# Two-dimensional Fourier mixing and an RWKV channel mix on one core: an earlier load gate and a new order of batch 1's loads

## The chip, the cores and the metric

The kernel runs on one core of a Trainium2 chip. The metric is the time of one execution on the device in microseconds. Times are given as the median of several runs; one further execution is profiled, and all rows of profile and trace come from that one.

## The reference, cut to what matters

The input x has 8 batches of 3072 rows (sequence) and 256 columns. The first stage takes the real part of a Fourier transform over both axes; the second is an RWKV channel mix over the result.

```python
X = np.fft.fft(x, axis=1)
X = np.fft.fft(X, axis=2)
x = X.real.astype(np.float32)

x_prev = np.concatenate([np.zeros((B, 1, D)), x[:, :-1, :]], axis=1)
xk = mu_k * x + (1.0 - mu_k) * x_prev
xr = mu_r * x + (1.0 - mu_r) * x_prev
k = np.maximum(xk @ w_k, 0.0)              # w_k: 256 x 1024
v = k * k @ w_v                            # w_v: 1024 x 256
r = 1.0 / (1.0 + np.exp(-(xr @ w_r)))      # w_r: 256 x 256
return r * v
```

## The kernel before, in words

**The mixing stage.** The kernel works through the batches one by one. As the input is real, only about half of the transform has to be computed, and the mirrored half follows from it. For each batch and each half h of the rows, `load_xh(b, h)` brings x from memory twice: `load_p` (L136, and L133 for batches from 2 on) brings rows in their order into a tile `xp`, and `load_m` (a gather by row numbers, L139, through the helper `gather`) brings the mirrored rows into `xm`. Half 0 has one more small gather of its own, `load_m0`. `fold(b, h)` (L168 and L170, on DVE) adds the two into `p`. Then come matrix products with tables of cosines and sines: `a_sum` (L574), or `butterfly` on DVE (L179) with `a_item` behind it (L533, L530); `d_units` (L596); `turned` (L619); `c_sums` (L637). They give `y`, the spectrum of the batch.

**The channel mix.** `diff` (L690) forms the difference of neighbouring rows, and `mix_part` or `mix` (L702, L713, L729, and L885 for the very first piece) forms the mixed inputs: `x00` and `x01` for K (first and mirrored half of the rows) and `x10`, `x11` for R. A batch has six chunks of 512 rows, three for each half m. For each chunk there are four pieces `k_piece` (PE, L748, with the relu on ACT, L758), squares (DVE, L768, or ACT, L766), `r_item` (PE, L775, with the sigmoid on ACT, L780), the second product (`v_part`, L801, for the first four chunks and `v_tile`, L789, after that), and `v_out` (DVE, L811), which multiplies by r and starts the stores on SP's queue (L819).

**The weights.** For half m of the rows the weights are `wk_sb[m]` (two tiles of 128x1024), `wr_sb[m]` (two of 128x256); `wv_sb` is shared. They are gathered by the row numbers in `row_i`, as the mirrored half needs them in another order of rows. `loads()` brings `wk_sb[0]` and `wv_sb`; `loads_1()` brings `wr_sb[0]`, and batch 1's two halves; `loads_2()`, called in step 4, makes the tables of row numbers for the later batches and brings `wk_sb[1]` and `wr_sb[1]`.

**What sets the order.** All loads named so far are issued from POOL's queue, in the order in which the program names them; POOL computes each load's list, so issuing takes it time too. Every engine's instructions run in the order of the program (`pin_order`). A list of steps is written out by hand: in step n PE gets one piece of K, then the step's other products, then parts of the second product; in the same step come the DVE work (`at(...)`) and the `v_out` that are due. Chunk 0 has the K pieces of steps 0 to 3, chunk 1 those of 4 to 7, and so on; `r_item` of chunk 0 stands in step 5, `fold(1, 0)` in step 4, `fold(1, 1)` in step 11, `v_part` of chunk 0 in steps 3 to 6, its `v_out` in step 6, `v_part` of chunk 1 from step 7. The second product has two slots of PSUM in all (`ps_v`), each of them for two blocks of 128 rows; `v_out` frees them. The other products share three slots (`ps_w`).

**The gate.** `load_gate` holds POOL's queue until DVE has come to a certain place: DVE sets one element to zero, and POOL's next instruction writes that element.

```python
def load_gate():
    V.memset(gate, 0)
    iota(gate, pattern=[[0, 1]], base=0, channel_multiplier=0)
```

So loads that the program names after the gate start no earlier than DVE's memset (L451) and POOL's iota (L452). Before the first gate, `loads()` has issued the first K weights and `wv_sb`; its `dma_start` is the last thing that POOL does until the gate.

`keep_busy(n, ps)` runs n products with zeros on PE; the numbers stand in `NF = (9, 0, 0, 3, 0, 3, 0)`, so that `NF[1]` and `NF[2]` are 0.

Of the kernel before, what the change touches and what calls it, by code (L numbers as in the profile page):

```python
# [20 lines left out]
def _v(ap, extra_offset, free_dims):  # L21
    new_ap = [list(ap.ap[0])] + [[s, c] for (s, c) in free_dims]
    return dataclasses.replace(ap, offset=ap.offset + extra_offset, ap=new_ap)
# [16 lines left out]
def kernel(  # L40
# [37 lines left out]
    def ps_w():  # L78
        return ps_slot("W", 3, 1024)

    def ps_v():
        return ps_slot("V", 2, 512)
# [35 lines left out]
    def x_tiles(b, h):  # L118
        xp_t[b, h] = xp_sb[(2 * b + h - 1) % 3] if b or h else xp_00
        xm_t[b, h] = xm_sb[(2 * b + h) % 3]  # L120
# [3 lines left out]
    def parts(b):  # L124
        return 112 if b > 1 else 96

    def load_p(b, h):
        r, n = 9 * h, 9 - h
        if b > 1:
            for g in range(2):  # L130
                src = dataclasses.replace(x[b, 32 * g + r:32 * g + r + 1, :],
                                          ap=[[64 * D, N1], [D, n], [1, D]])
                nc.gpsimd.dma_start(out=xp_t[b, h][64 * g:64 * g + N1, 0:n], in_=src)  # L133
            return
        src = dataclasses.replace(x[b, r:r + 1, :], ap=[[32 * D, 96], [D, n], [1, D]])
        nc.gpsimd.dma_start(out=xp_t[b, h][0:96, 0:n], in_=src)  # L136

    def gather(dst, src, idx):
        nc.gpsimd.indirect_dma_start(dst, None, src, bass.IndirectOffsetOnAxis(ap=idx, axis=0))  # L139

    def load_m(b, h, o, n, idx):
        gather(xm_t[b, h][0:parts(b), XM0 + o:XM0 + o + 256 * n],
               x.rearrange("b (s r) d -> (b s) (r d)", r=n), idx)

    def load_m0(b):
        if b == 0:
            gather(xm_00[:, 1:257], x.rearrange("b s d -> (b s) d"), idx_0[:, 0:1])
        else:
            load_m(b, 0, 2048, 1, (idx_g0 if b > 1 else idx_0)[:, b:b + 1])

    def load_xh(b, h):
        x_tiles(b, h)
        load_p(b, h)
        if h == 0:
            load_m0(b)
        load_m(b, h, 0, 8, (idx_g8 if b > 1 else idx_8)[:, b, h:h + 1])

    def fold(b, h, q0=0, n=0):

        n = n or 9 - h  # L160
        if (b, h) not in p_t:
            p_t[b, h] = p_pool.tile([112, 9, 256], FP16, name="p")
        k = parts(b)
        p, xp, xm = p_t[b, h][0:k], xp_t[b, h][0:k], xm_t[b, h][0:k]
        o = XM0 + 256 * (8 - h - q0)
        if (b, h, q0) == (0, 0, 0):
            xm, o = xm_00, 1
        V.tensor_tensor(out=p[:, q0:q0 + n], in0=xp[:, q0:q0 + n],  # L168
                        in1=_v(xm, o + 256, [(-256, n), (-1, 256)]), op=ALU.add)
        V.tensor_tensor(out=p[:, q0:q0 + n, 0], in0=xp[:, q0:q0 + n, 0],  # L170
                        in1=_v(xm, o, [(-256, n)]), op=ALU.add)
# [28 lines left out]
    def keep_busy(n, ps, cols=512):  # L200

        for _ in range(n):
            nc.tensor.matmul(out=ps[:, 0:cols], lhsT=zeros,
                             rhs=_v(zeros, 0, [(0, cols // P), (1, P)]), start=True, stop=True)

    fill = ps_w()
    keep_busy(4, fill)
    NF = (9, 0, 0, 3, 0, 3, 0)
# [72 lines left out]
    def rv(n, o, *dims, k=1):  # L281
        return _v(rw_0[0:k], P * n + o, list(dims)) if n < 6 else _v(rw_1, P * (n - 6) + o, list(dims))
# [45 lines left out]
    def outer(out, *pairs):  # L328
        for n, (row, r) in enumerate(pairs):
            nc.tensor.matmul(out=out, lhsT=row, rhs=r, start=n == 0, stop=n == len(pairs) - 1)  # L330
# [45 lines left out]
    ang_ps = [ps_v(), ps_v()]  # L376
# [46 lines left out]
    def rows():  # L423
        for a in range(2):
            for half in range(2):
                iota(_v(row_i[64 * half:64 * half + 64], a, [(3 - 2 * a, 2)]), pattern=[[0, 2]],
                     base=256 * a + half * (1 - 2 * a), channel_multiplier=2 - 4 * a)
        iota(row_i[0:1, 2:3], pattern=[[0, 1]], base=0, channel_multiplier=0)
        iota(_v(row_i[0:1], 1, [(2, 2)]), pattern=[[0, 2]], base=128, channel_multiplier=0)
# [11 lines left out]
    def loads():  # L441
        rows()
        for a in range(2):
            gather(wk_sb[0][a], moe_w_k, row_i[:, a:a + 1])
        nc.gpsimd.dma_start(out=wv_sb, in_=moe_w_v.rearrange("(fc p) v -> p fc v", p=128))
# [4 lines left out]
# [3 lines that stand above are left out]

    def loads_1():
        load_gate()
        for a in range(2):
            gather(wr_sb[0][a], moe_w_r, row_i[:, a:a + 1])
        load_xh(1, 0)
        load_xh(1, 1)

    def loads_2():
        for lo in (0, 64):
            k = slice(lo, 64 if lo == 0 else 112)
            iota(idx_g8[k], pattern=[[S // 8, B], [-1, 2]], base=S // 8 - 1 - lo // 16,
                 channel_multiplier=-8)
            iota(idx_g0[k], pattern=[[S, B]], base=S - lo // 2, channel_multiplier=-64)
        iota(idx_g0[0:1], pattern=[[S, B]], base=0, channel_multiplier=0)
        for a in range(2):
            gather(wk_sb[1][a], moe_w_k, row_i[:, 2 + a:3 + a])
        for a in range(2):  # L470
            gather(wr_sb[1][a], moe_w_r, row_i[:, 2 + a:3 + a])

# [36 lines left out]
    def evac(out_ap, in_ap, eng):  # L509
        if eng == "V":  # L510
            V.tensor_copy(out=out_ap, in_=in_ap)
        else:
            nc.scalar.activation(out=out_ap, in_=in_ap, func=AF.Copy)  # L513

    def a_tile(b):
        a_t[b] = y_pool.tile([P, 2, NU, 64], FP16, name="a")
# [45 lines left out]
    def a_sum(b, h, i0, eng="A", m=4):  # L562


        if (h, i0) == (0, 0):
            a_tile(b)
        ps = ps_w() if m == 4 else ps_v()
        for i in range(m):
            parts = [(h, i0 + i + 1 - h, 0, 2 * WA, 0, 1)]
            if h and i0 + i == 7:  # L570
                parts = [(0, 0, 0, WA, WA, 1), (1, 7, 1, WA, 1, 2)]
            for half, q, o, n, w, step in parts:
                for k in range(2):
                    nc.tensor.matmul(out=_v(ps, 256 * i + o, [(2 * WA // n, n)]),  # L574
                                     lhsT=p_t[b, half][0:96, q, 128 * k:128 * k + 128],
                                     rhs=_v(w_pm[0:96], (WA + WB) * k + w,
                                            [(WA + WB, 2), (step, n // 2)]),
                                     start=(k == 0), stop=(k == 1))
        a_ps[b, h, i0] = ps
        if eng:  # L580
            a_evac(b, h, i0, eng, m)
# [3 lines left out]
    def a_evac(b, h, i0, eng, m=4):  # L585
        evac(_v(a_t[b], 8 * h + i0, [(16, 2 * WA), (1, m)]),
             _v(a_ps[b, h, i0], 0, [(1, 2 * WA), (256, m)]), eng)
# [12 lines left out]
    def d_evac(ps, u0, n, bank, eng):  # L600
        evac(_v(g_all, 256 * u0, [(64, 2), (128, 2 * n), (1, 64)]),
             _v(ps, 0, [(bank, 2), (64, 2 * n), (1, 64)]), eng)
# [234 lines left out]
        outer(mu_ps[:, 4 + n:5 + n], (tv(TO + n, 0, (1, P)), rv(ONE, 0, (1, 1))))  # L837
    for k in range(2):
        outer(mu_ps[:, 64 + NU * k:64 + NU * k + NU], (rw_h[:, k], rv(JR, 0, (1, NU))))
    a_sum(0, 0, 0)  # L840
    fold(0, 0, 5, 4)
    a_sum(0, 0, 4)
    half_tables(mu_ps)
    V.tensor_copy(out=muf_t, in_=mu_ps[:, 0:6])
    loads()
    fold(0, 1, 0, 4)
    a_sum(0, 1, 0, "A")
    fold(0, 1, 4, 4)
# [8 lines left out]
    fill = ps_w()  # L857
# [16 lines left out]
    turned(2, 4, small[1][:, 256:258], "V")  # L874
    d_evac(fill[:, 256:1024], 4, 1, 512, "A")
    d_evac(fill[:, 384:1024], 5, 1, 512, "V")
    x_t[0, 0, 0] = mix_pool.tile([P, 2, 1536], FP16, name="x00")
    for a in range(2):
        t = x_t["t", a] = mix_pool.tile([P, 24, 64], FP16, name=f"t{a}")
# [3 lines left out]
    for a in range(2):  # L883
        for z in range(2):
# [2 lines left out]
                                   scalar=mu_f[:, a, 0:1],  # L887
                                   in1=_v(x_t["t", a], 64 * z, [(128, 2), (1, 64)]),
                                   op0=ALU.mult, op1=ALU.add)
    loads_1()  # L890
    y, odd = y_t[0], ps_v()
    even = ps_v()
    for f in range(2):
# [60 lines left out]
    event(3, (turned, 8, 13))  # L954
    event(4, (c_item, 0, 17, 8))
    at(4, loads_2)
    at(4, fold, 1, 0)
    at(5, r_item, (0, 0, 0))
# [158 lines left out]
```

## Time and profile before

| | us |
|---|---|
| median of 3 runs | 437.23 |
| lowest and highest run | 435.13 and 437.72 |
| the profiled execution | 439.32 |
| its span in the trace | 437.2 |
| PE busy | 425.7 (97%) |
| DVE busy | 361.5 (83%) |
| ACT busy | 321.6 (74%) |
| POOL busy | 63.8 (15%) |

The profile is of one execution. PE is TensorE's products and PEld its weight loads, DVE is VectorE, ACT is ScalarE, POOL is GpSimd, SP only issues DMAs here. Rows of the timeline have the start, the length in us, the engine, the line of the kernel, the operation, what it writes and reads, and how often; in brackets stands how long the engine had been idle before it, and what ended that. A row can stand for several instructions of one kind. The chain of waits is followed back from the last instruction of the stretch to what released it, step by step. In the windows each row is a stretch of time with the busy time of each engine in it (and the number of instructions), then the clock that TensorE was granted as a share of the full one, the busy share of the DMA engines and what they moved.

The mean granted clock of the whole execution was 0.992.

### The profile page before, as it was taken

The numbers are of one execution on the slowest core, as the hardware profiler recorded it, in microseconds if no ns is written. First come the engines' busy times: TensorE is split into PE (matmuls) and PEld (weight loads), VectorE is DVE, ScalarE is ACT, GpSimd is POOL, SyncE is SP. The second block draws the span as 40 slices with busy tenths as digits, with TensorE's granted clock in tenths as the row PEclk, the third lists the DMA queues.
The fourth block names the chain that finished last, engine by engine and source line by source line (L and its number), as shares of the span: only waits on it lengthen the run. The fifth ranks groups of instructions, "written<-read, shape, count | busy, mean of one in ns | idle before, by whom it ended". The sixth has DMA issues, their size and how long they took to land.

```text
span 437.2 us, 9304 instructions
## 1 busy us (share of the span) xinstructions
PE 425.7 (97%) x3853; PEld 299.7 (69%) x3853; DVE 361.5 (83%) x560; ACT 321.6 (74%) x375; POOL 63.8 (15%) x89
## 2 busy tenths in 40 slices
PE   8897999999999999999999999999999999999996
PEld 3564776777677777677767767776777776767675
DVE  8769889988898988989799888989889847997543
ACT  7695888787877777786787778777777867666661
POOL 7288401000041000500014000410000000000000
PEclk9898999999999999999999999999999999999999
DMA  7889953633259222863339332682322323233333
GB/s 133 118 132 194 202 99 58 120 73 73 49 111 190 60 56 68 143 148 69 71 58 189 94 73 62 111 189 50 70 63 64 70 53 72 52 71 73 73 73 97
DMA packets 34990, 41.81 MB, mean 96 GB/s; under 512 B 4098, under 2 KB 31076, under 8 KB 34948
## 3 DMA queue, kind: packets, MB, share of 16 engines
q1 hardware_dynamic: 27380, 24.92, 23.4%
q0 software_dynamic: 7264, 16.04, 22.6%
q8 instruction: 30, 0.49, 0.5%
q10 hardware_dynamic: 304, 0.26, 0.2%
q14 instruction: 12, 0.10, 0.1%
HBM read 32.08 MB, written 25.17 MB: 131 GB/s over the span
## 4 chain that ended last, share of the span: by engine, by line
PE 91%; DMA 3%; DVE 2%; POOL 1%; issue 1%; ACT 0%; DVEq 0%; ACTq 0%
PE psW L748 37%; PE psV L789 36%; PE psW L775 9%; DMA xm<-in_x_dram,idx 3%; PE psW L596 2%; PE psV L801 2%; PE psW L669 1%; PE psW L556 1%; PE psW L574 1%; PE psW L637 0%; DVE p L168 0%; POOL xm L139 0%; POOL wr L139 0%; PE psV L574 0%; DVE k L768 0%
## 5 line engine op out<-in xcount | busy, mean ns | idle before, releaser
L758 ACT ACTIVATE rl<-psW 128x1024 f16<-128x1024 f32 x192 | 195.3, 1025 | 95.7 <-PE psW L748 91.9
L748 PE MATMUL psW<-x,wk 128*128 128x512 f16 (+1 forms) x776 | 196.3, 378 | 0.5
L789 PE MATMUL psV<-wv_sb,k 128*128 128x256 f16 x1424 | 184.1, 273 | 0.0
L789 PEld LDWEIGHTS <-k 128*128 128x128 f16 x1424 | 136.9, 98 | 35.7
L768 DVE TENSOR_TENSOR k<-rl 128x2048 f16<-128x2048 f16 (+1 forms) x101 | 116.2, 1151 | 33.5 <-ACT rl L758 33.0
L748 PEld LDWEIGHTS <-wk 128*128 128x128 f16 x776 | 75.1, 98 | 54.0 <-issue 1.8
L811 DVE SCALAR_TENSOR_TENSOR o<-psV,r 128x512 f32<-128x512 f32 (+1 forms) x97 | 65.7, 680 | 16.0 <-PE psV L789 13.5
L713 DVE TENSOR_TENSOR x<-y,t 128x1536 f16<-128x1536 f16 (+2 forms) x72 | 61.6, 860 | 2.1
L775 PE MATMUL psW<-wr,x 128*128 128x256 f16 x384 | 49.8, 273 | 0.0
L780 ACT ACTIVATE r<-psW 128x1024 f16<-128x1024 f32 x48 | 48.9, 1019 | 0.8 <-PE psW L775 0.8
L775 PEld LDWEIGHTS <-x 128*128 128x128 f16 x384 | 37.5, 98 | 14.3 <-issue 0.2
L452 POOL IOTA gate<- 1x1 int32 x6 | 2.1, 356 | 205.1 <-DVE gate L451 205.1
L513 ACT ACTIVATE a<-psW 128x832 f16<-128x832 f32 x31 | 26.1, 863 | 3.2 <-PE psW L574 1.8
L139 POOL DMA_INDIRECT xm<-in_x_dram,idx_g x18 | 26.2, 1455 | 5.5 <-issue 5.2
L513 ACT ACTIVATE g_all<-psW 128x1024 f16<-128x1024 f32 (+5 forms) x37 | 25.6, 695 | 0.4 <-PE psW L619 0.2
L168 DVE TENSOR_TENSOR p<-xp,xm 112x2304 f16<-112x2304 f16 (+5 forms) x19 | 21.0, 1106 | 4.7 <-DMA xm<-in_x_dram,idx 4.7
L702 DVE TENSOR_SCALAR t<-d,muf_t 128x1536 f16<-128x1536 f16 (+2 forms) x40 | 20.7, 528 | 0.0
L702 DVE TENSOR_SCALAR t<-d,mu_m 128x1536 f16<-128x1536 f16 x32 | 19.6, 613 | 0.0
L801 PE MATMUL psV<-wv_sb,k 128*128 128x256 f16 x112 | 15.7, 283 | 3.0 <-DVE o L811 3.0
L596 PEld LDWEIGHTS <-a 128*128 128x128 f16 x208 | 14.1, 98 | 6.4 <-issue 0.4
L179 DVE TENSOR_TENSOR eo<-p 112x1152 f16<-112x1152 f16 (+3 forms) x28 | 17.8, 678 | 0.0
L513 ACT ACTIVATE pq<-psW 128x1024 f16<-128x1024 f32 (+1 forms) x18 | 15.2, 879 | 2.3 <-PE psW L669 2.3
(138 smaller groups left out, 221.3 us busy)
## 6 DMA issues: line engine op xcount, KB each, us to landing
out_dram<-o SPq DMA_DIRECT2D x189, 128.0 KB, 2.4
xp<-in_x_dram POOLq DMA_DIRECT2D x12, 216.0 KB, 4.6
xp<-in_x_dram POOLq DMA_DIRECT2D x12, 192.0 KB, 7.1
xp<-in_x_dram POOLq DMA_DIRECT2D x2, 432.0 KB, 5.2
xp<-in_x_dram POOLq DMA_DIRECT2D x2, 384.0 KB, 7.2
wv_sb<-in_moe_w_v_dram POOLq DMA_DIRECT2D x1, 512.0 KB, 8.2
xm<-in_x_dram,idx_g POOLq DMA_INDIRECT x18, 8.0
out_dram<-o ACTq DMA_DIRECT2D x1, 128.0 KB, 2.9
```

What stands on the lines that cost most here:

```text
L139: nc.gpsimd.indirect_dma_start(dst, None, src, bass.IndirectOffsetOnAxis(ap=idx, axis=0))
L513: nc.scalar.activation(out=out_ap, in_=in_ap, func=AF.Copy)
L702: V.tensor_scalar(out=dst, in0=src, scalar1=mu, scalar2=None, op0=ALU.mult)
L713: V.tensor_tensor(out=_v(x_t[b, j, m], o, [(64 * step, hi - lo), (step, 64)]), in0=y_t[b][:, lo + 3 * m:hi + 3 * m, a], in1=x_t["t", a][:, ...
L748: nc.tensor.matmul(out=st["k", ds][:, 512 * hs + lo:512 * hs + hi], lhsT=wk_sb[m][a][:, 128 * fc:128 * fc + 128], rhs=xk[:, a, 512 * i + l ...
L758: nc.scalar.activation(out=st["rl"][:, 2 * ds:2 * ds + 2], in_=st["k", ds].rearrange("p (f t) -> p f t", f=2), func=AF.Relu, bias=0.0, sca ...
L768: V.tensor_tensor(out=k2_t[c][:, lo:hi], in0=r, in1=r, op=ALU.mult)
L775: nc.tensor.matmul(out=ps[:, 256 * tb:256 * tb + 256], lhsT=x_t[b, 1, m][:, a, 512 * i + 128 * tb: 512 * i + 128 * tb + 128], rhs=wr_sb[m] ...
L780: nc.scalar.activation(out=st["r", c], in_=ps, func=AF.Sigmoid)
L789: nc.tensor.matmul(out=st["v", tb - h][:, 256 * h:256 * h + 256], lhsT=k2_t[c][:, fc, 128 * tb:128 * tb + 128], rhs=wv_sb[:, fc], start=(f ...
L801: nc.tensor.matmul(out=st["v", tb - h][:, 256 * h:256 * h + 256], lhsT=k2_t[c][:, fc, 128 * tb:128 * tb + 128], rhs=wv_sb[:, fc], start=fc ...
L811: V.scalar_tensor_tensor(out=o.rearrange("p a b -> p (a b)")[:, 0:256 * n], in0=st["v", t0][:, 0:256 * n], scalar=16.0, in1=st["r", c][:, ...
```

## The change

The first gate and batch 1's first half are issued ahead of the first mix (the `scaled` pieces on ACT and the four operations of L885 on DVE) instead of behind it. Within that, `load_xh(1, 0)` stands ahead of the gathers of `wr_sb[0]`. `load_xh(1, 1)` moves from there into `loads_2`, between the gathers of `wk_sb[1]` and those of `wr_sb[1]`. Two calls of `keep_busy` with the numbers `NF[1]` and `NF[2]` are added, which issue nothing, as both numbers are 0. The order of the instructions on PE and ACT stays the same; on DVE only the gate's memset moves, ahead of L885; POOL has the same instructions in the new order.

```diff
     def loads_1():
         load_gate()
+        load_xh(1, 0)
         for a in range(2):
             gather(wr_sb[0][a], moe_w_r, row_i[:, a:a + 1])
-        load_xh(1, 0)
-        load_xh(1, 1)
 
     def loads_2():
...
         for a in range(2):
             gather(wk_sb[1][a], moe_w_k, row_i[:, 2 + a:3 + a])
+        load_xh(1, 1)
         for a in range(2):
             gather(wr_sb[1][a], moe_w_r, row_i[:, 2 + a:3 + a])
...
+    keep_busy(NF[1], fill)
     a_sum(0, 0, 0)
...
     loads()
+    keep_busy(NF[2], ang_ps[1])
     fold(0, 1, 0, 4)
...
     d_evac(fill[:, 256:1024], 4, 1, 512, "A")
     d_evac(fill[:, 384:1024], 5, 1, 512, "V")
+    loads_1()
     x_t[0, 0, 0] = mix_pool.tile([P, 2, 1536], FP16, name="x00")
...
                                    op0=ALU.mult, op1=ALU.add)
-    loads_1()
     y, odd = y_t[0], ps_v()
```

## The prediction

> **What bounds the kernel now.** I read the page first: how busy each engine is over the whole span.
>
> ```profile
> span 437.2 us, 9304 instructions
> PE 425.7 (97%) x3853; PEld 299.7 (69%) x3853; DVE 361.5 (83%) x560; ACT 321.6 (74%) x375; POOL 63.8 (15%) x89
> ```
>
> PE has work in 425.7 of 437.2 us, so an edit that only moves loads can win no more than the 11.5 us in which PE is idle, and what a lowered TensorE clock costs beside them. Where that is, the chain of waits tells. I took it for 9 to 66 us, the stretch in which batch 1's loads are issued and used; it is followed backwards from the end, so every row in it set the time of the row after it.
>
> ```profile
> 20.17 1.12 DVE x L885 x4
> ...
> 21.39 0.12 POOL gate L452
> ...
> 21.68 0.98 POOL wr L139
> ...
> 22.97 0.99 POOL wr L139
> ...
> 23.97 0.59 POOL xp L136
> ...
> 26.21 6.44 DMA xm<-in_x_dram,idx
> ...
> 32.77 1.37 DVE p L168
> ...
> 37.67 0.61 DVE o L811
> ...
> 38.33 1.87 PE psV L801 x8
> ...
> 41.62 0.87 PE psV L801 x8
> ```
>
> The columns are start, length, what. The reader sees the very things that the change moves: the first mix (L885), the gate, the two gathers of R's weights (`wr`), then batch 1's first half (xp, and two gathers into xm), whose last gather lands 6.44 us after its issue began; `fold(1, 0)` (L168) waits for it; behind the fold on DVE is `v_out` of chunk 0 (L811), and PE's `v_part` of chunk 1 (L801) waits for that. The timeline gives the idle times at the three places:
>
> ```profile
> 27.78 1.28 DVE L768 TENSOR_TENSOR k<-rl 128x1024 f16<-128x1024 f16 x2
> 32.77 1.35 DVE L168 TENSOR_TENSOR p<-xp,xm 96x2304 f16<-96x2304 f16 x1 [3.71 <-DMA xm<-in_x_dram,idx]
> 33.38 1.04 PE L801 MATMUL psV<-wv_sb,k 128*128 128x256 f16 x8
> 34.25 1.03 PE L748 MATMUL psW<-x,wk 128*128 128x512 f16 x4
> 38.33 1.87 PE L801 MATMUL psV<-wv_sb,k 128*128 128x256 f16 x8 [3.05 <-DVE o L811]
> ```
>
> DVE is free at 27.78 + 1.28 = 29.06 and stands 3.71 us before the fold. PE is free at 34.25 + 1.03 = 35.28 and stands 3.05 us. The windows show what follows that stop, and which stretches have DMA room:
>
> ```profile
> 20.00:22.00 2.00, 1.87 (x27) 1.25 (x26) 1.83 (x7) 1.47 (x5) 0.44 (x2) 1.00 0.08 11
> ...
> 35.40:38.30 2.90, 0.00 (x0) 0.00 (x0) 2.87 (x11) 1.99 (x2) 2.60 (x4) 0.91 1.13 183
> 38.30:40.00 1.70, 1.68 (x9) 1.17 (x9) 1.70 (x6) 0.00 (x0) 1.40 (x2) 0.50 0.97 152
> 40.00:41.70 1.70, 1.70 (x8) 0.76 (x7) 1.70 (x6) 0.04 (x1) 1.70 (x1) 0.65 1.01 197
> 41.70:437.00 395.30, 391.27 (x3603) 279.00 (x3600) 328.33 (x427) 291.82 (x317) 36.10 (x44) 1.00 0.43 91
> ```
>
> Busy times are PE, PEld, DVE, ACT, POOL; then granted clock, DMA share, GB/s. After the stop the clock is 0.50, then 0.65 on the mean; from 41.7 us on it is 1.00 and PE works 391.27 of 395.30 us. So time won before 41.7 us has almost nowhere to be lost again. From 20 to 22 us the DMA engines are nearly idle (0.08), though batch 1's loads could run there: the gate holds them.
>
> **The change part by part.** No instruction is added or removed; all is order.
>
> The gate. Its one DVE memset moves ahead of the four L885 operations.
>
> ```profile
> 19.43 0.41 DVE L511 CAST g_all<-psW 128x256 f16<-128x256 f32 x1
> 20.17 1.12 DVE L885 SCALAR_TENSOR_TENSOR x<-psW,muf_t,t 128x128 f16<-128x128 f32 x4 [0.33 <-ACT t L880]
> 21.24 0.06 DVE L451 MEMSET gate<- 1x1 int32 x1
> ```
>
> DVE ends the cast at 19.84 and then waits 0.33 us for ACT, so the memset of 0.06 us fits into that wait and costs nothing; without that cover it would delay the first mix by 0.06 us. It starts at about 19.84 in place of 21.24, so POOL's iota moves from 21.39 to about 19.98: 1.4 us.
>
> The order behind it. xp followed the two `wr` gathers, 23.97 - 21.68 = 2.29 us of POOL's time; now it follows the iota. xp's issue moves from 23.97 to about 20.27 (3.7 us earlier), and the last xm gather, which came 2.24 us behind it, from 26.21 to 22.5. With the same 6.44 us to landing it lands at 28.95 instead of 32.65, so the fold can start at about 29.06, when DVE is free: the 3.71 us are gone. The landing can be other than that from both sides. The rows for it:
>
> ```profile
> wr<-in_moe_w_r_dram,row_i POOLq DMA_INDIRECT x2, 2.7
> wr<-in_moe_w_r_dram,row_i POOLq DMA_INDIRECT x1, 5.9
> xm<-in_x_dram,idx POOLq DMA_INDIRECT x1, 8.1
> DMA to landing us min/median/max: 2.7/6.2/10.0
> ```
>
> They are the times to landing of issues in three windows (21 to 23, 33 to 34.5, 29 to 31 us) and of all gathers of L139. At the shortest 2.7 us xm lands at 25.2 and nothing more is won, as DVE is not free earlier. At the 8.1 us of the next half's gather it lands at 30.6 and the fold still waits 1.55 us. I take 6.44, the row of the same transfer; it had `wr` ahead of it and the next half right behind it, and now has neither that close.
>
> What PE then waits for. DVE's work from the fold to the first `v_out` moves by 3.71 us: `v_out` could start at 37.67 - 3.71 = 33.96, but it reads what PE and ACT give it:
>
> ```profile
> 30.44 1.04 PE L775 MATMUL psW<-wr,x 128*128 128x256 f16 x8
> 31.68 1.28 ACT L780 ACT_TABLE_LOAD   x1
> 32.98 1.02 ACT L780 ACTIVATE r<-psW 128x1024 f16<-128x1024 f32 x1
> 36.37 1.06 ACT L766 ACTIVATE k<-rl 128x1024 f16<-128x1024 f16 x1
> 41.66 1.02 ACT L758 ACTIVATE rl<-psW 128x1024 f16<-128x1024 f32 x1 [4.23 <-PE psW L748]
> ```
>
> r is there at 34.00 and the first half of psV's eight matmuls (33.38 + 1.04 = 34.42 for all) at about 33.9. So the two `v_out` of 0.61 to 0.66 us run from about 34.05 to 35.35, and PE, free at 35.28, finds its first slot released at 34.7 and the second one about when it comes to it. I leave 0.05 us of the 3.05.
>
> The clock. From 38.33 to 41.62 the chain has eight L801 and four L748 in 3.29 us; the same pair at full clock is 33.38 to 34.25 and 34.25 to 35.12 by the starts and lengths above, 2 x 0.87 = 1.74. So the stop cost another 1.55 us. Without the stop that goes too; if only the stop shrinks, it may stay. ACT would not hold PE: its square at 36.37 ends at 37.43, and the next `rl` has then been ready since about 37.0, with 4.23 us of ACT idle to give and three psW slots between the two.
>
> The Trainium skill ("TensorE: Matmul & The Clock Gate", The HAM clock gate) has the clock halved after at least one idle window of about 3.4 us. By that rule a stop of 3.05 us would leave the clock alone, and the change would win 3.0 us, 434.2.
>
> The rows here speak otherwise: a stop of 1.47 us earlier in the kernel was enough.
>
> ```profile
> 13.49 1.22 PE L574 MATMUL psW<-w_pm,p 96*128 96x208 f16 x8 [1.47 <-DVE p L170]
> 14.50:15.50 1.00, 1.00 (x8) 0.80 (x7) 0.87 (x7) 0.74 (x1) 0.00 (x0) 0.50 0.87 92
> ```
>
> After it the granted clock is 0.50 as well, so I count the 1.55 us.
>
> What becomes later. `wr` now goes behind xm: xm's issue lasts from 22.5 to 23.7, and the second `wr` starts at about 25.3 in place of 22.97. PE first reads it at 30.44 (L775, `r_item` of step 5). Landing took 2.7 us with empty queues and 5.9 us behind the second K gathers, so it is there at 28.0 to 31.2: hidden, or a stop of PE of up to 0.8 us. I take it as hidden, since the queue ahead of it is done with xm at about 28.95 and `wr` needs little more. ACT's r would not be late with either: it waits for ACT's table load, 31.68 to 32.96, while L775 ends at 31.48. The bound beyond these rows is the 10.0 us maximum, 35.3 (the second rival).
>
> Batch 1's second half moves behind the iotas and the two second K gathers. These rows give its last gather, POOL's iotas and K gathers (from the first of these rows' IOTA to the `wr` behind them), and the fold that uses it:
>
> ```profile
> 28.32 1.55 POOL L139 DMA_INDIRECT xm<-in_x_dram,idx  x1 [0.30 <-issue]
> 29.87 0.20 POOL L464 IOTA idx_g<- 64x16 uint32 x1
> ...
> 33.34 1.60 POOL L139 DMA_INDIRECT wr<-in_moe_w_r_dram,row_i  x1 [0.31 <-issue]
> ...
> 48.31 1.22 DVE L168 TENSOR_TENSOR p<-xp,xm 96x2048 f16<-96x2048 f16 x1
> ```
>
> Its issue at 28.32 moves by -3.7 for the start, +2.3 for the two `wr` and 33.34 - 29.87 = +3.5 for iotas and K gathers, to 30.4. At the fold DVE is at most 4.5 us earlier, 43.8, and even with 10.0 us to landing the data is there at 40.4: 3.4 us of cover. The second K weights are issued earlier than now, by the 1.4 us of the gate and POOL's time for batch 1's second half (1.55 us for its gather alone) that no longer stands ahead of them; the second R weights and all of batch 2 behind them come 1.4 us earlier, and batch 2 is folded only in step 17. SP's queue has no loads in it. These edits cost nothing.
>
> The sum, against the profiled execution's own 439.32 us (span 437.2): 3.05 - 0.05 + 1.55 = 4.55 us, and I take 4.5: span 432.7, 434.8 for such an execution. The median of the runs shown is 437.23, practically this span, so the same 4.5 us give **432.7 us**.
>
> **The rivals.** First, the stop only shrinks: xm takes 8.1 us to land, the fold is 1.55 us late, the first `v_out` ends at 38.28 - 2.16 = 36.1, PE stands 0.85 us and wins 2.2 us, with the clock's 1.55 lost or not: 435.0 to 433.5, say 434.5. For it: the DMA share is about 1 from 35 us on (1.13, 0.97). Against it: the queues are empty at 20 to 22 us.
>
> Second, the other side: `wr` becomes the wait. PE runs in order, so `r_item` at 30.44 would hold `v_part`, every later K product and ACT's r. It decides from a landing at about 33.5, as a stop of 3.05 us there returns all that is won. At the 10.0 us maximum it lands at 35.3, PE stands 4.86 us and pays the clock again: -4.55 + 4.86 + 1.55 = +1.9, **439.1 us**. Slower by 1% it would be with a landing over 12 us. For it: xm's 96 gathered rows are just ahead in the same queue. Against it: the `wr` behind the K gathers took 5.9 us. The Trainium skill ("DMA: Bandwidth & Descriptors", Queues, rings and completion order) says that each DMA engine consumes descriptors in ring order; by that `wr` could not overtake xm and would land just behind xm's 28.95, close to PE's 30.44 but ahead of it, so the sum stays.
>
> Third, the clock comes back by itself: the stop goes, but the half clock had another cause, or falls on another stretch: 3.0 us, 434.2. Against it: the clock is 1.00 before the stop and after 41.7 us.
>
> Fourth, the change doesn't do what it says: the landing is set by the bytes that the DMA engines can move and not by the issue, and xm still lands at 32.65: 437.2. Against it again the 0.08 of DMA share just where the loads would go.
>
> **How the numbers follow.** Forecast 0.70, shrunk stop 0.09, `wr` 0.08, clock 0.07, no effect 0.06. A measurement of this kernel can tell about 1% (4.4 us) from no change, and the forecast is just past that, at 432.86; the runs before spread over 2.6 us, so I put 0.44 of its 0.70 past it and 0.26 short. Within 1%: 0.26 + 0.09 + 0.07 + 0.06 and 0.03 of `wr`, 0.51, slower by over 1% the other 0.05. The range goes from 431.0 (all of it, and a run as low beside the median as the lowest was) to 436.8, which takes in the shrunk stop and the clock and leaves out no effect and `wr`.
>
> **What would show it.** Right: the gate's iota at about 20.0; xp's issue straight behind it; `fold(1, 0)` at 29.1 with no idle time of DVE before it from DMA; the L801 group after L748's step 7 starts at about 35.3 with no wait over 0.3 us; ACT's 4.23 us gone; clock 1.00 between 37 and 42 us; all later rows about 4.5 us earlier. Wrong: a PE or PEld wait for `wr` at L775 near 30.4; a wait of the second fold near 44; a wait of the first fold over 1 us; or a half clock at a place that had none.

## The result and the profile after

| | before | changed |
|---|---|---|
| median of 22 runs, us | 437.43 | 434.18 |
| lowest and highest run, us | 435.13 to 442.92 | 433.0 to 437.3 |
| profiled execution, us | 439.32 | 433.00 |
| its span, us | 437.2 | 430.9 |

The ratio of the runs is 0.9937, 95% interval [0.9918, 0.9956]: the change takes 0.6% off, 2.7 us. The forecast was 432.7 us in a range of 431.0 to 436.8. The two profiled executions lie 6.3 us apart, more than twice as much. Which of the two is the change?

The timeline of the changed kernel, the same stretch as before (start, length, engine, line, operation; in brackets the idle time ahead of it):

```profile
18.22 0.12 POOL L452 IOTA gate<- 1x1 int32 x1 [4.02 <-DVE gate L451]
18.44 0.57 POOL L136 DMA_DIRECT2D xp<-in_x_dram  x1
18.45 1.13 DVE L888 SCALAR_TENSOR_TENSOR x<-psW,muf_t,t 128x128 f16<-128x128 f32 x4 [0.33 <-ACT t L883]
...
20.58 0.93 POOL L139 DMA_INDIRECT xm<-in_x_dram,idx  x1 [0.30 <-issue]
...
26.06 1.29 DVE L768 TENSOR_TENSOR k<-rl 128x1024 f16<-128x1024 f16 x2
27.53 1.35 DVE L168 TENSOR_TENSOR p<-xp,xm 96x2304 f16<-96x2304 f16 x1 [0.19 <-DMA xm<-in_x_dram,idx]
28.72 1.04 PE L775 MATMUL psW<-wr,x 128*128 128x256 f16 x8
32.37 1.29 DVE L811 SCALAR_TENSOR_TENSOR o<-psV,r 128x512 f32<-128x512 f32 x2
32.53 1.03 PE L748 MATMUL psW<-x,wk 128*128 128x512 f16 x4
33.39 1.04 PE L801 MATMUL psV<-wv_sb,k 128*128 128x256 f16 x8
```

The fold's wait for xm has gone from 3.71 to 0.19 us, and PE's L801 follows L748 with no wait at all. This execution reached `r_item` 1.72 us earlier than the first one; with that added, the gate's iota stands at 19.94, the fold at 29.25 and L801 at 35.11 us, where the prediction had about 20.0, 29.1 and 35.3. The windows (PE, PEld, DVE, ACT, POOL, clock, DMA share, GB/s) show the full clock behind it, and a stretch at the start, 14 to 15 us:

```profile
14.00:15.00 1.00, 1.00 (x11) 0.89 (x11) 0.72 (x7) 1.00 (x2) 0.20 (x1) 1.00 0.66 80
35.40:38.30 2.90, 2.90 (x26) 2.22 (x24) 2.83 (x7) 2.87 (x4) 2.87 (x3) 1.00 1.13 199
```

The 6.3 us come apart by two fixed points. `r_item` of step 5 (L775) stands at 30.44 before and 28.72 after: 1.72 us were won ahead of it, where the change does nothing to PE. There the first profile had a wait of 1.47 us and a half clock behind it (0.50 at 14.5 us, shown in the prediction); this one has full clock. So that part is one execution against another: two more profiles of the kernel before, shown below, reach `r_item` at 28.30 and 28.70. Behind it, the chain's L801 of step 8 stands at 41.62 before and, in this chain of waits, here:

```profile
35.29 0.87 PE psV L801 x8
```

That is 6.33 us, of which 4.61 arise between the two points; the forecast had 4.55. From this point to the end it is 395.58 us before and 395.61 after. So between this execution and the one that the sum was worked out from, the predicted mechanism did very nearly the predicted amount, and nothing was lost later; but the medians lie 3.25 us apart and the ratio says 2.7. The experiments are about that gap, and about which part of the change does it.

### The profile page after: what moved, and what is told of

The parts are those of the page before. It is cut to its first block, busy times and chain, and to the rows that moved or that the text cites. A ratio compares the mean times of both kernels' runs of the same rounds, so it can differ in the third digit from the quotient of the medians.

```text
span 430.9 us, 9304 instructions
## 1 busy us (share of the span) xinstructions
PE 423.0 (98%) x3853; PEld 298.2 (69%) x3853; DVE 361.4 (84%) x560; ACT 321.5 (75%) x375; POOL 61.0 (14%) x89
## 4 chain that ended last, share of the span: by engine, by line
PE 94%; ACT 2%; DMA 1%; POOL 1%; DVE 1%; issue 1%; ACTq 0%; POOLq 0%
PE psW L748 38%; PE psV L789 36%; PE psW L775 10%; PE psV L801 3%; PE psW L596 2%; PE psW L669 1%; PE psW L556 1%; DMA xm<-in_x_dram,idx 1%; ACT rl L758 1%; POOL xm L139 1%; PE psW L637 1%; PE psW L574 0%; ACT g_all L513 0%; DVE x L888 0%; PE psV L574 0%
## 5 line engine op out<-in xcount | busy, mean ns | idle before, releaser
L748 PE MATMUL psW<-x,wk 128*128 128x512 f16 (+1 forms) x776 | 195.6, 377 | 0.5
L789 PE MATMUL psV<-wv_sb,k 128*128 128x256 f16 x1424 | 184.1, 273 | 0.0
L748 PEld LDWEIGHTS <-wk 128*128 128x128 f16 x776 | 74.9, 98 | 53.6 <-issue 1.3
L775 PE MATMUL psW<-wr,x 128*128 128x256 f16 x384 | 49.8, 273 | 0.0
L775 PEld LDWEIGHTS <-x 128*128 128x128 f16 x384 | 37.5, 98 | 14.3 <-issue 0.2
L139 POOL DMA_INDIRECT xm<-in_x_dram,idx_g x18 | 24.4, 1356 | 5.5 <-issue 5.5
L690 DVE TENSOR_TENSOR d<-y 128x1664 f16<-128x1664 f16 (+5 forms) x19 | 16.7, 879 | 0.0
```

Of the source, the lines that this page charges most:

```text
L748: nc.tensor.matmul(out=st["k", ds][:, 512 * hs + lo:512 * hs + hi], lhsT=wk_sb[m][a][:, 128 * fc:128 * fc + 128], rhs=xk[:, a, 512 * i + l ...
L775: nc.tensor.matmul(out=ps[:, 256 * tb:256 * tb + 256], lhsT=x_t[b, 1, m][:, a, 512 * i + 128 * tb: 512 * i + 128 * tb + 128], rhs=wr_sb[m] ...
L789: nc.tensor.matmul(out=st["v", tb - h][:, 256 * h:256 * h + 256], lhsT=k2_t[c][:, fc, 128 * tb:128 * tb + 128], rhs=wv_sb[:, fc], start=(f ...
```

## The experiments

All ratios are to runs of the kernel before on the same chip, whose median was 437.07 us beside the first four experiments, 438.06 beside the last two and 436.53 beside the others; a ratio is not simply the quotient of two medians. The mean granted clock of each run is used too. In the first profile the clock is at about half in two stretches of 3.4 us (13.8 to 17.2 and 37.8 to 41.2 us), and its mean is 0.992; so, as an estimate from these figures, one such stretch in a run of 435 us gives a mean of 0.996.

**Only the gate.** The old `loads_1()`, unchanged, called at the new place:

```diff
+    loads_1()
     x_t[0, 0, 0] = mix_pool.tile([P, 2, 1536], FP16, name="x00")
...
-    loads_1()
     y, odd = y_t[0], ps_v()
```

> The kernel before with only the gate (and all that is behind it, in the old order: R's weights, batch 1's first half, its second half) ahead of the first mix. Theory A (the gain is the stop of PE behind the fold, in each execution, and the half clock that follows it): all of POOL's loads come 1.4 us earlier, the fold's wait on DVE falls from 3.7 to 2.3 us, PE's stop from 3.05 to about 1.6 us, the half clock stays: 1.4 us faster, about 436.0, ratio 0.997. Theory B (the profiled execution of before was one of the slower ones, and in most executions the stop costs little or the clock does not fall behind it): the wait of the fold is shorter too, but the time moves by under 0.7 us. Rival C (landing is set by the DMA engines and not by the issue): the fold's wait stays at 3.7 us.

Measured: 434.96 us, ratio 0.9964 [0.9936, 0.9992]. Its timeline:

```profile
29.75 1.36 DVE L168 TENSOR_TENSOR p<-xp,xm 96x2304 f16<-96x2304 f16 x1 [1.20 <-DMA xm<-in_x_dram,idx]
35.30 1.20 PE L801 MATMUL psV<-wv_sb,k 128*128 128x256 f16 x8 [0.54 <-DVE o L811]
```

The wait shrank, against rival C, and the ratio is theory A's; but the wait is 1.20 us and not 2.3, the stop 0.54 and not 1.6. Earlier by 1.4 us from a wait of 3.7 doesn't give 1.20; from about 2.6 it does, if this execution was one with a shorter landing.

**Only the order.** The new `loads_1()` and `loads_2()`, with the old place of the call; against the changed kernel:

```diff
-    loads_1()
     x_t[0, 0, 0] = mix_pool.tile([P, 2, 1536], FP16, name="x00")
...
+    loads_1()
     y, odd = y_t[0], ps_v()
```

> The kernel before with only the new order (batch 1's first half ahead of R's weights, its second half behind the second K weights), the gate behind the first mix as before. Theory A: the fold's gather is issued 2.3 us earlier, the fold's wait falls from 3.7 to 1.4 us, PE's stop to about 0.7 us; 2.3 us faster with the half clock still there, 3.8 us without it, as a stop of 0.7 us leaves PE at work in most of the time: 433.6 to 435.1, ratio 0.991 to 0.995. Theory B: less than 1.5 us faster. Rival C: wait of 3.7 us as before.

Measured: 433.64 us, ratio 0.9936 [0.9906, 0.9966]. Its fold stands without any wait:

```profile
28.35 1.35 DVE L168 TENSOR_TENSOR p<-xp,xm 96x2304 f16<-96x2304 f16 x1
```

The order alone does what the whole change does (0.9937), within the intervals. 2.3 us of earlier issue were expected to leave 1.4 us of wait and left none; xm landed in 5.1 us in this execution, where the prediction had 6.44. Once there is no wait, the gate's 1.4 us have nothing to shorten; whether they help in executions with a later landing isn't shown.

**Nothing loaded earlier, the fold later.** In the kernel before, with the fold and its butterfly moved:

```diff
-    at(4, fold, 1, 0)
...
-    at(7, butterfly, 1, 0, 1)
...
+    at(8, fold, 1, 0)
+    at(8, butterfly, 1, 0, 1)
     at(8, half_scale)
```

> The kernel before with no load moved, but fold(1, 0) moved from step 4 to step 8 and its butterfly from step 7 to behind it, so that the squares, the mix and v_out that stood behind the waiting fold on DVE run ahead of it. Theory A (what counts is what stands behind the fold in DVE's queue, not the load): no wait for DMA on DVE, PE's stop at step 7 gone, clock full behind it: 4 to 4.5 us faster in the profile, as much as the changed kernel, ratio 0.990 to 0.994. Theory B: as much as the changed kernel in the median of the runs too, 2.8 us (0.9937). Rival (the early loads help by themselves, by their landing or by less DMA traffic later): well short of the changed kernel, under 1 us.

Measured: 435.33 us, ratio 0.9968 [0.9939, 0.9998]: faster, but by about half of what was expected (0.990 to 0.994). The profile:

```profile
34.36 1.29 DVE L811 SCALAR_TENSOR_TENSOR o<-psV,r 128x512 f32<-128x512 f32 x2 [0.51 <-ACT r L780]
37.57 1.35 DVE L168 TENSOR_TENSOR p<-xp,xm 96x2304 f16<-96x2304 f16 x1
43.78 1.28 DVE L811 SCALAR_TENSOR_TENSOR o<-psV,r 128x512 f32<-128x512 f32 x2
44.52 1.20 PE L801 MATMUL psV<-wv_sb,k 128*128 128x256 f16 x8 [0.43 <-DVE o L811]
```

The wait for DMA is gone and so is the stop at step 7. So what stood behind the fold in DVE's queue was the cost, as the theory has it, since no load is issued earlier. But a new stop of 0.43 us comes at step 11, as `v_out` of chunk 1 starts at 43.78 us with no idle time of DVE ahead of it: DVE is at work for 9.28 of the 9.42 us from the first `v_out` to here, and the moved fold and butterfly now stand ahead of the second one. So the edit brings some of the cost to another place. From `r_item` of step 5 to the end this profile takes 402.8 us and the changed kernel's 402.2, the difference being 0.6 us; why the median is 1.7 us above that of the order alone is not shown beyond that.

**The stop filled.** In the kernel before:

```diff
+        if step == 7:
+            keep_busy(14, ps_w())
         if step in p_steps:
             v_part(*p_steps[step])
```

> The kernel before with 14 products with zeros of 512 columns (3.0 us at full clock) on PE between step 7's K piece and v_part of chunk 1, just where PE stops; nothing else is changed. The stop stays, filled. Theory A (the half clock is the stop's, 1.55 us in each execution): v_part starts at about the same 38.3 us, the clock stays 1.00 behind it, 1.5 us faster, about 435.9, ratio 0.9965. Theory B (the clock does not fall behind the stop in most executions): under 0.5 us in the median, while the profile may show it. Rival (the clock falls for another reason): the same half clock, 0 us or some tenths slower for products beyond the stop's end.

Measured: 437.25 us, ratio 1.0007 [0.9985, 1.0028]. The profile says why:

```profile
31.62 1.36 DVE L168 TENSOR_TENSOR p<-xp,xm 96x2304 f16<-96x2304 f16 x1 [2.60 <-DMA xm<-in_x_dram,idx]
35.07 3.19 PE L203 MATMUL psW<-zeros 128*128 128x512 f16 x14
36.44 1.27 DVE L811 SCALAR_TENSOR_TENSOR o<-psV,r 128x512 f32<-128x512 f32 x2
38.09 1.04 PE L801 MATMUL psV<-wv_sb,k 128*128 128x256 f16 x8
```

The first `v_out` ends at about 37.1, the products only at 38.1: they were cut for the first profile's stop and are 1 us too long for this one. Clock 1.00 behind them, and no gain. This can't settle how often the clock falls; but the fold's wait here is 2.60 us, and that is the second sign that 3.71 us was a long one.

**The kernel before, profiled twice more.** Nothing changed.

> The kernel before, unchanged, one more profiled execution. Theory (the first profile was an execution with a late landing): the wait of the fold is 2.3 to 2.9 us rather than 3.71 and PE's stop 1.8 to 2.3 us rather than 3.05; where the mean clock is 1.00 the clock behind the stop is 1.00 too. Rival (the first profile was typical, and the size is lost elsewhere): wait of 3.5 us and more, stop of 3 us.

> The kernel before, unchanged, another profiled execution, with the same expectations: wait of the fold 2.3 to 2.9 us, stop of PE 1.8 to 2.3 us by the theory of a late landing in the first profile; 3.5 and 3 us by its rival.

The first took 434.64 us, the second 437.49. The first one's fold, stop and the window behind the stop:

```profile
29.33 1.36 DVE L168 TENSOR_TENSOR p<-xp,xm 96x2304 f16<-96x2304 f16 x1 [2.41 <-DMA xm<-in_x_dram,idx]
34.88 1.19 PE L801 MATMUL psV<-wv_sb,k 128*128 128x256 f16 x8 [1.75 <-DVE o L811]
34.88:38.00 3.12, 3.12 (x22) 2.14 (x22) 3.12 (x11) 1.42 (x2) 2.51 (x3) 1.00 1.05 139
```

The same of the second:

```profile
30.57 1.35 DVE L168 TENSOR_TENSOR p<-xp,xm 96x2304 f16<-96x2304 f16 x1 [3.24 <-DMA xm<-in_x_dram,idx]
36.11 1.61 PE L801 MATMUL psV<-wv_sb,k 128*128 128x256 f16 x8 [2.58 <-DVE o L811]
38.00:39.00 1.00, 1.00 (x4) 0.40 (x3) 1.00 (x5) 0.00 (x0) 1.00 (x1) 0.50 0.90 161
```

So the same program has a stop of 1.75, 2.58 or 3.05 us, with the clock at 1.00 behind it once and at 0.50 twice. xm's landing took 5.1, 6.0 and 6.4 us in the three. The first of the two new ones is about as the theory has it, the second lies between the theory and its rival. The first profile's stop was the longest seen.

**Only the second half moved.** The kernel before with `load_xh(1, 1)` behind the second K gathers:

```diff
         load_xh(1, 0)
-        load_xh(1, 1)
...
+        load_xh(1, 1)
         for a in range(2):
             gather(wr_sb[1][a], moe_w_r, row_i[:, 2 + a:3 + a])
```

> The kernel before with only batch 1's second half moved behind the second K weights; gate and R's weights as before. Theory (the landing is set by the issue): batch 1's first half is issued at the same time, the fold's wait stays at 2.6 to 3.7 us, the time stays at 437.1. Rival (the second half's transfers, right behind, share the DMA engines and hold up the first half's last bytes): xm lands up to 1.5 us earlier, the wait falls by as much, 1 to 1.5 us faster, ratio about 0.997.

Measured: 436.29 us, ratio 0.9985 [0.9947, 1.0024], a wait of 2.51 us at the fold and a stop of 1.85. Both lie within what the kernel before shows by itself: this part moves nothing that can be measured, and a gain under 0.4% is left open.

**R's weights behind the second K weights.** The changed kernel with

```diff
         load_xh(1, 0)
-        for a in range(2):
-            gather(wr_sb[0][a], moe_w_r, row_i[:, a:a + 1])
...
+        for a in range(2):
+            gather(wr_sb[0][a], moe_w_r, row_i[:, a:a + 1])
         load_xh(1, 1)
```

> The changed kernel with the gathers of wr_sb[0] moved behind those of the second K weights: 3.5 us later on POOL, issued from about 25.3 and 26.6 us in the time of the changed kernel's profile, and with 5 us to landing there at about 31.6. r_item of step 5 on PE is due at 28.7. The cover of wr in the changed kernel (from about 1 to 3 us by the prediction's bounds) is then gone. Theory (PE runs in order, so wr's landing becomes the stop): PE waits about 2 to 3 us at L775, what is won is lost: 436 to 437, ratio to before 0.997 to 1.000. Rival (wr overtakes, or lands in 3 us): a wait under 1 us, under 0.5 us slower than the changed kernel.

Measured: 439.89 us, ratio 1.0069 [1.0029, 1.0108], the slowest kernel of the study:

```profile
30.70 0.27 PE L775 MATMUL psW<-wr,x 128*128 128x256 f16 x1 [1.32 <-DMA wr<-in_moe_w_r_dram,row_i]
32.80 0.93 PE L775 MATMUL psW<-wr,x 128*128 128x256 f16 x7 [1.83 <-DMA wr<-in_moe_w_r_dram,row_i]
34.40:37.80 3.40, 3.40 (x14) 1.81 (x13) 0.00 (x0) 1.38 (x3) 2.75 (x4) 0.50 1.14 202
38.01 1.29 DVE L811 SCALAR_TENSOR_TENSOR o<-psV,r 128x512 f32<-128x512 f32 x2 [5.30 <-PE psV L801]
```

PE stands 1.32 + 1.83 us for `wr`, a half clock follows, and `v_out` waits for PE. This is the prediction's second rival, brought about by another order: wait for wait it costs more than the stop that the change removed. The median was expected at 436 to 437 us; it came out about 3 us above that.

**Products at the start.** The changed kernel with `NF[2] = 3`, and with `NF[1] = 2` and `NF[2] = 5`; the edit of the first:

```diff
-    NF = (9, 0, 0, 3, 0, 3, 0)
+    NF = (9, 0, 3, 3, 0, 3, 0)
```

> The changed kernel with NF[2] = 3: three products with zeros of 512 columns (0.65 us at full clock) where PE waits for the last of batch 0's gathers at 12 to 13.5 us. Theory: what spreads the changed kernel's runs (433.6 us where the mean granted clock is 0.998 or more, 436 where it is 0.991) is a half clock after the waits of PE at 11 to 14 us, in some executions only. Products in that wait would keep the clock: the runs at 435 us and above become rarer, the median goes down by 0.3 to 0.8 us from 434.2, the fastest runs stay at 433.0 to 433.5. Rival (the half clock comes from elsewhere, the main loop for one): the same share of slow clocks, median the same or up to 0.4 us later.

> The changed kernel with NF[1] = 2 and NF[2] = 5: products with zeros in both of PE's waits at 9 to 14 us (0.43 and 1.1 us at full clock). Theory as for three products, and more of it: hardly a run under a mean clock of 0.995; but in executions whose gathers land early the products run past the end of the wait, up to 0.6 us: fastest runs at 433.3 to 434.0, median about 433.8. Rival (the half clock comes from elsewhere): the same share of slow clocks and the median 0.5 us later.

Measured: 433.57 us, ratio 0.9916 [0.9885, 0.9946], and 433.51 us, ratio 0.9904 [0.9865, 0.9942]. Of 19 runs one had a mean clock under 0.998, where the changed kernel had 10 of 22, in another group of runs. Two rows of the second kernel's profile: the products, and PE's next work, with no wait between them.

```profile
12.54 1.24 PE L203 MATMUL psV<-zeros 128*128 128x512 f16 x5
13.86 0.89 PE L574 MATMUL psW<-w_pm,p 96*128 96x208 f16 x8
```

**The same products in both kernels.** The kernel before with three products at that place, and the changed kernel with three again, on one chip.

> The kernel before with the same three products with zeros in PE's wait at 12 us as in the changed kernel with NF[2] = 3, loads as before. Theory (two things make up the spread of the kernel before: a half clock at the start, which the products take away, and the stop of 1.75 to 3.05 us at 33 to 38 us, with a half clock behind it where the stop is long): median about 435.7, about 1.3 us faster than before; some runs at a mean clock of 0.996 left, from the stop, hardly any at 0.992. Rival (the half clock that the products took away was not the start's): as before, 437.1, same share of slow clocks.

> The changed kernel with NF[2] = 3 again, on the same chip as the kernel before with the same products. Theory (with the start's half clock out of both, what is left between the two is the stop, about 2 us, and the half clock that follows it in some executions): 433.6 median again, 2.0 to 2.7 us below the other. By the prediction's size (stop 3.05 us and 1.55 us of half clock in each execution) the two would lie 4.5 us apart.

Measured: 436.43 us, ratio 0.9975 [0.9949, 1.0001], and 435.0 us, ratio 0.9922 [0.9899, 0.9945]; the medians are 1.4 us apart, the means of the runs, 436.74 and 434.64, 2.1 us. Expected were 435.7 and 433.6 us, 2.0 to 2.7 apart: both came out higher, and only the means have that distance. By neither are they the 4.5 us of the prediction's size apart. Of the 12 runs of the former none has a mean clock under 0.994 and 6 have 0.994 to 0.996; of the 22 runs of the kernel before on this chip 7 have 0.992 or less. So the products take the slowest clocks away from the kernel before too, though its gain in time is not clear of noise. Its profile has a long stop with full clock behind it:

```profile
36.49 1.20 PE L801 MATMUL psV<-wv_sb,k 128*128 128x256 f16 x8 [2.66 <-DVE o L811]
37.00:38.00 1.00, 1.00 (x8) 0.62 (x7) 1.00 (x5) 0.00 (x0) 0.70 (x2) 1.00 1.25 236
```

And the changed kernel's with products shows what is late next, in step 11:

```profile
43.85 0.69 DVE L811 SCALAR_TENSOR_TENSOR o<-psV,r 128x512 f32<-128x512 f32 x1 [1.54 <-DMA out_dram<-o]
44.59 0.60 PE L801 MATMUL psV<-wv_sb,k 128*128 128x256 f16 x4 [0.73 <-DVE o L811]
```

The median of 435.0 is higher than the 433.57 of the same kernel on another chip. Its runs at a clock of 0.998 and more lie in two groups, 433.1 to 433.9 and 434.5 to 435.3; this profile (its execution took 435.06) belongs to the upper one. What makes the upper group is not shown. The wait for the store is the smaller part even here: of the 2.0 us between the spans of this profile and the changed kernel's, about 0.45 are lost ahead of L801 of step 3, 0.9 between that and `r_item` of step 9, where PE's longest waits are 0.15 and 0.20 us for ACT's `rl` and `r`, and 0.73 at this store. The two profiles with products on the other chip have the same wait of DVE, 0.79 and 0.78 us, and no wait of PE behind it.

## Why the prediction was right, and where its size was off

**The mechanism was right, step by step.** The gate's memset was hidden in DVE's 0.33 us wait, xp's issue follows the gate's iota, the fold has (almost) no wait, L801 follows without a stop, the clock stays at 1.00. The two half changes agree: each shortens the wait, by as much as its share of issue time can take off the 2.4 to 3.7 us of the kernel before, and the order alone is enough. Moving the fold instead of the loads shows that DVE's order is what turned a late load into a stop of PE. From `r_item` of step 5 to the end, four profiles with the old order of loads and the fold in its old place (three of the kernel before, one with products at the start) take 404.2, 405.0, 406.7 and 406.8 us; five with the new order (the changed kernel, the order alone, three with products at the start) take 402.0 to 403.2. So in the profiles the new order is worth 1.0 to 4.8 us behind that point, 3.3 on the mean.

**The term that was mis-sized is the stop with its clock, 3.05 + 1.55 us.** The prediction took it from one execution and carried it over to the median ("so the same 4.5 us give"). That execution took 439.32 us, 2.1 us over the median of the runs, and that was the warning: it was an execution that had lost more than usual. Three profiles of the same program gave stops of 1.75, 2.58 and 3.05 us; the mean is 2.5. Among runs whose mean clock is 0.998 or more, so that no half clock of length is in them, the kernel before has a median of 435.4 us (29 of 85 runs) and the changed one 433.6 (12 of 22): 1.8 us for the stop without the clock, if these runs have the same stops as the others. The rest to 2.7 is about 0.9 us, and that is where the clock and all else must lie: 1.55 us was the price in one execution, not in each.

**How far the range and the number are luck.** 432.7 us was 1.5 us too low. The range held 434.18 because it had been set to take in a stop that only shrinks and a half clock with another cause, not because their sizes were known. And 434.2 stands in the prediction twice, for 3.0 us won and no price for the clock: where it speaks of a clock that the stop leaves alone, and in the third rival. That the median comes out there bears out neither. The stop was under 3.05 us in all but one of the four profiles with the old order and a stop, and the half clock did follow it in two of them. Other terms happen to give the same number.

**The clock was taken as given by the stop, and is not.** A stop of 2.58 us was followed by a clock of 0.50, one of 2.66 us by 1.00. The Trainium skill ("TensorE: Matmul & The Clock Gate", The HAM clock gate) says that the clock follows windows of about 3.4 us that run freely and don't start with the work; these two rows agree with a fall that depends on where the stop lies and not on its length alone. Its other statement, that a whole idle window of about 3.4 us is needed, doesn't hold here: 2.58 us were enough, and 1.47 us at the start.

**The spread was another thing.** Much of what differs from run to run is a half clock at the start. It stands in the first profile and in those of the late fold, the filled stop and the moved half, and not in the two other profiles of the kernel before. No profile of a kernel with the new order has it; that it comes there too is concluded from the 10 of 22 runs with a mean clock under 0.998, and from the products at the start, which make such runs rare. The prediction saw its row and used it only as evidence for the price.

**`wr` had less cover than given as likely.** Its second gather began at 23.16 and these rows of the changed kernel's DMA issues (the last number is us to landing; the windows are 23 to 24 and 20.5 to 21 us) put it at 28.2, and xm at 27.4:

```profile
wr<-in_moe_w_r_dram,row_i POOLq DMA_INDIRECT x1, 5.0
xm<-in_x_dram,idx POOLq DMA_INDIRECT x1, 6.8
```

L775 starts at 28.72: 0.5 us of cover. It landed 0.8 us behind xm, close to what the prediction's argument against its second rival had. But the order in which descriptors are consumed, on which that argument rests, is not yet an order of landing: that a later load can't overtake is shown by no run here.

**The first rival is partly there.** xm took 6.8 us to land and not 6.44, so the fold still waits 0.19 us, which costs PE nothing: L801 follows L748 without a wait.

**A new wait was in none of the rivals.** `v_out` has three output tiles, and a store has to land before its tile is written again. The earlier `v_out` starts its stores while batch 2's loads are in the queues. Rows of the DMA issues for 8 us around the first four stores (the last number is the median us to landing), in the kernel before (37 to 45 us), the changed one (32 to 40) and the changed one with three products in the last experiment (32 to 40):

```profile
out_dram<-o SPq DMA_DIRECT2D x4, 128.0 KB, 4.3
```

```profile
out_dram<-o SPq DMA_DIRECT2D x4, 128.0 KB, 7.2
```

```profile
out_dram<-o SPq DMA_DIRECT2D x4, 128.0 KB, 11.1
```

From 4.3 to 7.2 us costs the changed kernel 0.18 us of DVE's time in its profile and PE nothing; at 11.1 us it is the wait of 1.54 us shown above, with 0.73 us of PE's time behind it. So time won before 41.7 us could be lost again, against the prediction's sentence on that.

## What to carry to other kernels

A load that is late costs what stands behind its reader in the reader's queue, so moving the reader, or only the order of the loads on the issuing queue, can do as much as starting all of it earlier. Before a stop is turned into a forecast, compare the profiled execution's own time with the median: if it is slower, its stops are too long for the median, and a second profile is worth more than a second decimal. The version to keep is the changed kernel with products in the waits of the start (433.5 us, 0.9904 [0.9865, 0.9942], and 0.9916 and 0.9922 with three products): below the kernel before in each group of runs, and with few half clocks left; that it beats the changed kernel itself is likely by the medians, but the intervals overlap.

## What the runs showed of the hardware that was not expected

The landing of one and the same gather took 5.1 to 6.4 us in three executions of one program. That of the first four stores took 4.3 to 11.1 us in three kernels, with other loads in the queues, where the median of all of the stores of the kernel before is 2.4 us; what share the other loads have in it is not shown. Half clocks come in some executions only, and behind short waits: 1.47 us in the first profile, and 0.64 and 0.81 us, one after the other, in that of the filled stop, where the clock is 0.54 on the mean between 15 and 16 us. Three products with zeros, 0.81 us of PE's time in the profiles, go with a share of runs with a mean clock under 0.998 of 3 in 23, where it was 10 in 22 without them, in other groups of runs.
